# First stored weight set loaded inside the last block, third chunk's attention outputs moved by half a slot, two token sums made elsewhere

## The chip, the cores and the metric

One core of a Trainium2 chip runs the kernel. The metric is device time in microseconds (us) of one execution; the kernel before was timed three times. A profile is one execution more, with the start and length of every instruction on TensorE (PE, and PEld for its weight loads), VectorE (DVE), ScalarE (ACT), GpSimd (POOL) and the DMA issues of SyncE (SP).

## What is computed

```python
x = attention(q, k, v)          # 4 batches x 8 heads x 576 tokens x 64; heads 0-3: window 32,
                                # heads 4-7: 32 keys at a stride of 4; softmax; fp32
x = x as (2304 tokens, 512)
h = x @ w_in                    # 512 -> 2048
x = (h * sigmoid(h)) @ w_out    # 2048 -> 512
a, b = x @ w1, x @ w2           # 512 -> 1024 each
out = ((a * b) @ w3) @ w_out2   # 1024 -> 1024 -> 512
```

## The kernel before

Every fp32 operand of a large product is kept as two parts, an upper half (ScalarE's rounded copy) and a lower half (VectorE's difference), and a product is three matmuls: upper by upper, lower by upper, upper by lower. Weights arrive as 64-bit patterns and are converted on the chip: SP loads a piece of 512 KB into one of four `raw` buffers, ScalarE re-biases it, VectorE puts the bits together (two operations), ScalarE makes the upper half, VectorE the lower one. Each engine, SP too, works through its instructions in the order in which the program lists them; the order is written out by hand.

The tokens of the first feed-forward part go in five chunks, `CH1`, of 512, 512, 256, 512 and 512. For chunks 1 to 3 a *slot* (the loop after L1187) does one of 16 feature blocks: it makes `h` of the next block in two halves (`h` and `H` in the strings of `SLOT`, L72), the tanh and the gating (`t`), the halves of the gated block (`g`), and the product of the present block with `w_out` in two halves (`x` and `X`). An `a` in the string is one step of the attention of a later batch, eight steps per two heads' pair of units: outputs and scores (V, S), maxima on VectorE (M), exponentials (E, E), sums, GpSimd's multiplication and the copies into `xT` (N, O, L), transposes (T), and their copies out of PSUM (W). A slot has the string of the half in which the next step falls. A `p` is one operation out of a list of sums, `todo`.

Chunks 4 and 5 are computed together as a two by two block product with seven products instead of eight (`HPROD`, `h_product`, L863), which needs four sums of token blocks, T1 to T4; `t_ops` (L821) lists the operations that make them: raw sums `whole` into `x_a` to `x_d`, differences `sub`, and upper and lower halves `high` and `low`. T4 comes from `x_d`, T3 from `x_c`. The list `early` may run during the third chunk's attention, `late` in its last slots (string `SLOT[2]`), `last_` after them. Then the loop at L1324 runs eight pairs of seven products; the first pair does them in the order 0, 2, 4, 1, 3, 5, 6, with the last block's two `x` halves and the store of the third chunk (`x2_store`) between them, and product 0 is copied out of its bank twice (L1345). Four banks take turns. T1 is read by the third product, T2 by the fourth, T3 by the fifth, T4 by the sixth. During the later pairs three *sets* of the second part's weights (upper and lower halves of seven blocks) are made and stored to memory (`set_ops`), each 1.75 MB in two pieces (1024 and 768 KB).

The *last block* (loop at L1369) has 16 places of 12 matmuls for chunk 5, with up to seven conversion steps at each place (`LATE_MICROS`). At place 6 the tokens of the second part are loaded (`load_x2`, four loads of 384 KB). Then `weights(k, part)` (L1395) computes the product of `w3` and `w_out2`, 16 groups for the first half of the columns (k = 0 to 7), each of two parts of six matmuls, while the weights for the next groups are loaded and converted. The stored sets are read back there, at the values of k in `SET_AT` (L78) by `set_io` (L518), which issues two loads; they overwrite the tiles `wf[0]` to `wf[5]`, whose contents the last block read in places 6 to 11. After k = 8 the second part's products (`product`, L1045) begin, on two banks that the last groups' splits (L490) free.

Of the kernel before, what the change touches and what calls it, by code (L numbers as in the profile page):

```python
# [8 lines left out]
F32 = mybir.dt.float32  # L9
# [8 lines left out]
P = 128  # L18
# [11 lines left out]
PER_B = NPAIR * NU  # L30
# [40 lines left out]
ATT = "V2S0|M0|E1|E0|N0O3|L1O2|T0|W0"  # L71
SLOT = (  # L72
    ("ahapHppaxptapgX", "ahappHpxaptaXpg"),
    ("ahaHtapxgpaX", "ahHpaxtgpXaap"),
    ("phpHtxgpXpp",) * 2,
)
LATE_MICROS = 7
SET_AT = (1, 3, 6)  # L78
GROUP = ("mmmmw", "mmmmW")
MICROS = ("2223332", "3332121")  # L80
LAST = "00 01 02 20 21 13 22 14 33 34 15 35".split()
# [9 lines left out]
def tile_kernel(  # L91
# [650 lines left out]
    def x2_part(c, f, half):  # L742
        n = CH1[c][1]
        if f == 0 and half == 0:
            xps[c] = [ps_x.tile([P, 512], F32, tag="x", name=f"x2_{c}_{m}") for m in range(KT)]
        g = gt[c, f] if half == 0 else gt.pop((c, f))
        if half == 0 and type(g) is tuple:
            g = g[0]
        todo = [(m, sa, 0) for m in range(KT) for sa in (0, 1)] + [(m, 0, 1) for m in range(KT)]
        for m, sa, sb in todo[6 * half:6 * half + 6]:  # L750
            nc.tensor.matmul(  # L751
                xps[c][m][:, :n], wout(f, sa, m), g[:, sb],
                start=(f == 0 and sa == 0 and sb == 0), stop=(f == NF - 1 and sb == 1),
            )
# [66 lines left out]
    def t_ops():  # L821

        def tmp(k):
            if k not in tmps:
                tmps[k] = rawp.tile([P, 2, 512], F32, tag="raw", name=f"x_{k}")
            return tmps[k]

        def whole(k, r, c, kt):
            nc.vector.tensor_add(tmp(k)[:, kt], f32(x_block(r, c, 0, kt)), f32(x_block(r, c, 1, kt)))

        def sub(k, x, y, kt):
            nc.vector.tensor_sub(tmp(k)[:, kt], tmp(x)[:, kt], tmp(y)[:, kt])

        def view(n, k, kt):
            x = tmp(k)[:, kt]
            return x.rearrange("p (a n) -> p a n", a=2) if n == 3 else x

        def high(n, k, kt):
            nc.scalar.activation(t_block(n, 0, kt), view(n, k, kt), AF.Copy)

        def low(n, k, kt):
            nc.vector.tensor_sub(t_block(n, 1, kt), view(n, k, kt), f32(t_block(n, 0, kt)))

        two = lambda op, *z: [lambda kt=kt: op(*z, kt) for kt in range(2)]
        early = two(whole, "a", 0, 0) + two(whole, "b", 0, 1) + two(sub, "a", "b", "a")
        late = (two(high, 1, "a") + two(whole, "c", 1, 1) + two(low, 1, "a") + two(sub, "a", "c", "a") + two(high, 2, "a")
                + two(whole, "d", 1, 0) + two(low, 2, "a") + two(sub, "d", "d", "a") + two(high, 4, "d")
                + two(sub, "c", "c", "b") + two(low, 4, "d"))
        last_ = two(high, 3, "c") + two(low, 3, "c")
        return early, late, last_  # L850

    HPROD = [("11", "11"), ("S2", "T2"), ("12", "21"), ("S3", "T3"), ("S1", "T1"), ("22", "T4"), ("S4", "22")]
# [120 lines left out]
    def load_x2(pr):  # L973
        for half in range(2):
            for blk in range(2):
                t = x2p.tile([P, 2, T2], F32, tag=f"xb{half}{blk}", name=f"xb_{pr}_{half}{blk}")
                t0 = (2 * pr + blk) * T2
                nc.sync.dma_start(
                    out=t, in_=x2d[2 * half * P:(2 * half + 2) * P, t0:t0 + T2].rearrange("(m p) t -> p m t", p=P)
                )  # L980
                xb[f"{half + 1}{blk + 1}"] = t
# [155 lines left out]
    with tc.manual_schedule():  # L1137
# [50 lines left out]
        for i, (c, f) in list(enumerate(slots))[NF:-1]:  # L1188
            nxt = slots[i + 1]
            half = att.half()  # L1190
            if att.at == len(att.steps) and "T" not in tmps:
                attn.close()
                parts_ = ctx.enter_context(ExitStack())
                sp = parts_.enter_context(tc.tile_pool(name="sp", bufs=1, side="right", reuse_waits="tile"))
                tmps["T"] = [sp.tile([P, 2, 2, 512], F32R, tag=f"T{n}", name=f"T{n}") for n in range(2)]
                for u in (1, 2, 3):
                    load_sw(0, u)
                todo += late
            for x in SLOT[2 if "T" in tmps else c - 1][half]:
                if x == "h":  # L1200
                    if nxt[1] == 0:
                        att.need(2)
                    h_part(*nxt, 0)
                elif x == "H":
                    h_part(*nxt, 1)
                    if nxt[1] == NF - 1:
                        att.limit = (c + 3) * PER_B
                elif x == "t":
                    g_tanh(*nxt)
                    g_mul(*nxt)  # L1210
                elif x == "g":
                    g_high(*nxt)
                    g_low(*nxt)
                elif x in "xX":
                    x2_part(c, f, "xX".index(x))
                    if x == "X" and f == NF - 1:
                        x2_store(c, (0, 2))
                elif x == "a":
                    if att.half() == half:
                        att.step()  # L1220
                elif x == "p" and todo and (len(todo) > len(early) or c == 2 and (att.out >= 3 * PER_B + 6 or "T" in tmps)):
                    todo.pop(0)()
        load_sw(0, 0)
        for op in todo + last_:
            op()

        def gate(c):
# [96 lines left out]
        for p in range(NP):  # L1324
            if p == 1:
                bank = [ps_x.tile([P, 512], F32, tag="x", name=f"hx{k}") for k in range(4)]
                xps[3] = [(ps_h if m < 2 else ps_a).tile([P, 512], F32, tag="h" if m < 2 else "a", name=f"x2_3_{m}")
                          for m in range(KT)]
            for j, i in enumerate((0, 2, 4, 1, 3, 5, 6) if p == 0 else range(7)):
                live[i] = bank[done[0] % 4]  # L1330
                done[0] += 1
                h_product(p, i, live[i])
                if p == 0 and j < 2:
                    x2_part(2, NF - 1, j)
                    if j == 1:
                        x2_store(2, (0, 2))
                        raws = [rawp.tile([P, 2, 512], F32, tag="raw", name=f"c_{k}") for k in range(2)]
                        cs.update(s1=raws[0][:, 0], u2=raws[0][:, 1], u3=raws[1][:, 0], c22=raws[1][:, 1])
                        o = rawp.tile([P, 2, 2, 256], F32, tag="raw", name="set_out")
                        w = rawp.tile([P, 512, 2], I32, tag="raw", name="set_raw")  # L1340
                        t = sp.tile([P, 256], F32, tag="set_t", name="set_t")
                        sets = [op for s in range(SETS) for op in set_ops(s, t, w, o)]
                        ts.append(gp.tile([P, 512], F32, tag="t", name="t_s", bufs=1))
                        for k in ("s1", "u3"):
                            nc.scalar.activation(cs[k], live[0], AF.Copy)  # L1345
                elif p == 0:
                    begin_h(i)
                else:
                    collect_h(p, i)
                x_some(3, xs, 4 if i < 3 else 3, NF - 1)  # L1350
                for _ in range(2 if i in (1, 2, 3, 5, 6) else 1):
                    if sets and p:
                        sets.pop(0)()
            xs = first_x(p)
# [14 lines left out]
        for i, f in enumerate(LATE):  # L1369
            for z in x_todo():  # L1370
                x_mm(4, f, g_late(f), *z, first_=i == 0, last=i == NF - 1)
            cv2.allowed = sum(z <= i for z in free_at)
            if i == 6:
                load_x2(0)
            if i >= 8 and begin:
                begin.pop(0)()
            for _ in range(LATE_MICROS):
                cv2.micro()
# [16 lines left out]
        def weights(k, part):  # L1395

            if (k, part) == (3, 0):
                x2_store(NC1 - 1, (2,))
            if part == 0:
                cv2.allowed = W3[min(k + 1, 2 * NG - 1)] + 1  # L1400
                cv2.need(W3[k])
                if k < NG:
                    cv2.need(WO[k], False)
                if k in SET_AT:
                    set_io(SET_AT.index(k), False)
            for x in GROUP[part]:
                if x == "m":
                    cv2.micro()
                else:
                    wp_group(k, part)  # L1410
                    if todo:
                        x_split(todo.pop(0))
# [108 lines left out]
```

## Time and profile before

| | |
|---|---|
| time, three runs | 798.47, 798.94 (median), 800.08 us |
| the profiled execution | 800.56 us, of which the span of the trace is 798.8 us |
| TensorE (matmul) busy | 784.3 us, 98% |
| VectorE busy | 557.8 us, 70% |
| ScalarE busy | 346.0 us, 43% |
| GpSimd busy | 55.8 us, 7% |
| DMA | 120.93 MB, 151 GB/s in the mean, 370 GB/s in the busiest of 40 slices (479 to 499 us) |

Busy times are sums over instructions. A TensorE matmul starts before the modelled end of the one before it, so that its busy time hides small gaps. The chain of waits of the page goes through TensorE for nearly all of the span.

### The profile page before, as it was taken

The numbers are of one execution on the slowest core, as the hardware profiler recorded it, in microseconds if no ns is written. First come the engines' busy times: TensorE is split into PE (matmuls) and PEld (weight loads), VectorE is DVE, ScalarE is ACT, GpSimd is POOL, SyncE is SP. The second block draws the span as 40 slices with busy tenths as digits, with TensorE's granted clock in tenths as the row PEclk, the third lists the DMA queues.
The fourth block names the chain that finished last, engine by engine and source line by source line (L and its number), as shares of the span: only waits on it lengthen the run. The fifth ranks groups of instructions, "written<-read, shape, count | busy, mean of one in ns | idle before, by whom it ended". The sixth has DMA issues, their size and how long they took to land. (4 is left out here: it accounts for less than half of the span.)

```text
span 798.8 us, 13328 instructions
## 1 busy us (share of the span) xinstructions
PE 784.3 (98%) x4829; PEld 678.5 (85%) x4829; DVE 557.8 (70%) x1334; ACT 346.0 (43%) x868; POOL 55.8 (7%) x90
## 2 busy tenths in 40 slices
PE   7999999999999999999999999999999999999997
PEld 6788888888889897888888887889899999999996
DVE  5998892776765657878874857588877555774444
ACT  6877873554545534444433645343233211320111
POOL 4101100010100100000000000013300000000000
PEclk9999999999999999999999999999999999999999
DMA  9787740524235103455434859518522660045202
GB/s 240 230 275 230 215 147 16 195 96 168 83 130 172 56 15 106 137 166 159 145 119 156 275 223 370 174 54 324 229 93 68 207 251 2 1 152 204 93 1 79
DMA packets 54562, 120.93 MB, mean 151 GB/s; under 512 B 5089, under 2 KB 25313, under 8 KB 52449
## 3 DMA queue, kind: packets, MB, share of 16 engines
q1 hardware_dynamic: 54208, 119.85, 45.3%
q8 instruction: 38, 0.62, 0.3%
q10 hardware_dynamic: 288, 0.23, 0.1%
q14 instruction: 28, 0.22, 0.1%
HBM read 87.56 MB, written 32.51 MB: 150 GB/s over the span
## 5 line engine op out<-in xcount | busy, mean ns | idle before, releaser
L1045 PE MATMUL bank<-xT,wf 128*128 128x384 f32 x864 | 164.0, 335 | 0.5 <-DVE wf L493 0.4
L1045 PEld LDWEIGHTS bank<-xT,wf 128*128 128x128 f32 x864 | 151.7, 188 | 7.7 <-DVE wf L493 0.8
L751 PE MATMUL x<-g,wf 128*128 128x512 f32 (+1 forms) x576 | 121.9, 357 | 1.5 <-ACT g L734 1.5
L711 PE MATMUL h<-xT,wf 128*128 128x512 f32 (+1 forms) x576 | 120.9, 358 | 0.0
L1101 PE MATMUL o<-wf,wf 128*128 128x512 f32 x429 | 110.0, 393 | 0.0
L751 PEld LDWEIGHTS x<-g,wf 128*128 128x128 f32 x576 | 95.1, 189 | 17.4 <-ACT g L734 2.2
L711 PEld LDWEIGHTS h<-xT,wf 128*128 128x128 f32 x576 | 95.1, 189 | 15.8
L1101 PEld LDWEIGHTS o<-wf,wf 128*128 128x128 f32 x429 | 79.5, 188 | 12.7
L1081 ACT ACTIVATE wf<-c 128x384 fp32r<-128x384 f32 x48 | 25.2, 525 | 84.9 <-DVE c L1079 84.6
L1063 ACT ACTIVATE s<-bank 128x384 f32<-128x384 f32 x24 | 11.8, 491 | 103.0 <-PE bank L1045 92.4
L885 PE MATMUL x<-ga,wf 128*128 128x512 f32 x192 | 51.9, 391 | 0.0
L729 DVE SCALAR_TENSOR_TENSOR t<-t,h 128x512 f32<-128x512 f32 (+1 forms) x48 | 28.6, 595 | 33.4 <-ACT t L725 33.0
L690 PE MATMUL wp<-wf,wf 128*128 128x512 f32 x192 | 46.9, 392 | 0.3 <-ACT wf L602 0.3
L265 ACT ACTIVATE sm<-sm,nm 128x96 f32<-128x96 f32 x108 | 39.1, 365 | 17.4 <-DVE nm L255 17.3
L725 ACT ACTIVATE t<-h 128x512 f32<-128x512 f32 (+1 forms) x48 | 25.1, 522 | 47.3 <-PE h L711 45.6
L885 PE MATMUL x<-wf 128*128 128x512 f32 x192 | 43.7, 389 | 0.0
L739 DVE TENSOR_TENSOR g<-t,g 128x512 fp32r<-128x512 f32 (+1 forms) x48 | 28.8, 600 | 20.3 <-ACT g L734 19.9
L280 POOL TENSOR_TENSOR sm<-sm,rs 128x288 f32<-128x288 f32 x36 | 27.2, 764 | 225.7 <-DVE rs L275 67.3
L885 PEld LDWEIGHTS x<-ga,wf 128*128 128x128 f32 x192 | 36.0, 188 | 8.1
L1070 DVE TENSOR_TENSOR c<-u,bank 128x384 f32<-128x384 f32 x36 | 19.9, 552 | 32.7 <-PE bank L1045 32.6
L885 PEld LDWEIGHTS x<-wf 128*128 128x128 f32 x192 | 36.0, 188 | 7.5
L690 PEld LDWEIGHTS wp<-wf,wf 128*128 128x128 f32 x192 | 35.7, 188 | 7.7 <-ACT wf L602 0.8
(168 smaller groups left out, 1214.3 us busy)
## 6 DMA issues: line engine op xcount, KB each, us to landing
rawj<-in_w_dram SPq DMA_DIRECT2D x26, 512.0 KB, 5.9
wf<-setd SPq DMA_DIRECT2D x11, 1024.0 KB, 5.3
wf<-setd SPq DMA_DIRECT2D x11, 768.0 KB, 7.0
raw_i<-in_w_in_dram SPq DMA_DIRECT2D x16, 512.0 KB, 4.6
raw_u<-in_w_out_dram SPq DMA_DIRECT2D x16, 512.0 KB, 4.6
swd<-sw SPq DMA_DIRECT2D x16, 512.0 KB, 2.6
sw<-swd SPq DMA_DIRECT2D x24, 256.0 KB, 3.2
setd<-set_out SPq DMA_DIRECT2D x21, 256.0 KB, 2.1
```

The costliest lines, as they stand in the source:

```text
L265: nc.scalar.activation(sm[:, j], sm[:, j], AF.Exp, bias=nm[:, j:j + 1], scale=-1.0, accum_out=su[:, j:j + 1],)
L280: nc.gpsimd.tensor_tensor(sm, sm, rs[:, :NB].to_broadcast([P, NB, KB]), op=ALU.mult)
L690: nc.tensor.matmul(wp_ps[i], a[:, i // 2, sa, i % 2 * P:(i % 2 + 1) * P], o[:, sb], start=(jt == 0 and x == 0), stop=(jt == NG - 1 and x = ...
L711: nc.tensor.matmul(ps, win(f, sa, kt), xT[:, kt, sb, r0:r0 + n], start=(kt == 0 and x == 0), stop=(kt == KT - 1 and x == 2),)
L725: nc.scalar.activation(gt[c, f], hps[c, f][:, :n], AF.Tanh, scale=0.5)
L729: nc.vector.scalar_tensor_tensor(t, t, 1.0, ps, op0=ALU.add, op1=ALU.mult)
L739: nc.vector.tensor_sub(g[:, 1], t, f32(g[:, 0]))
L751: nc.tensor.matmul(xps[c][m][:, :n], wout(f, sa, m), g[:, sb], start=(f == 0 and sa == 0 and sb == 0), stop=(f == NF - 1 and sb == 1),)
L885: nc.tensor.matmul(xps[c][m], wout(f, sa, m), g[:, sb], start=(first_ and sa == 0 and sb == 0), stop=(last and sb == 1),)
L1045: nc.tensor.matmul(b, a_op(s, a, sa, kt), b_op(x, sb, kt), start=(n == 0), stop=(n == 5),)
L1081: behind.append((count[0] + 1, lambda: nc.scalar.activation(hi, c[k], AF.Copy)))
L1101: nc.tensor.matmul(ps, g_block(jj, n, sa)[:, m % 3 * P:(m % 3 + 1) * P], wp_v(f, sb)[:, c0:c1], start=((first_ or len(parts) == 2) and x = ...
```

## The change

Four edits. In the third chunk's slots with attention, the outputs and scores stand after the first half of `h` instead of before it, and the maxima after the second half (`SLOT[1][0]`). T4's raw sum goes from `late` to `early`, T4's halves go from `late` to a list that runs after the first of the 56 products, and T3's difference moves forward in `late`; `SLOT[2]` has three `p` instead of five. The copies of the first product out of its bank, and the buffers for them, stand right after that product instead of after the third chunk's store. The first set is loaded at place 11 of the last block instead of at k = 1, the second at k = 1 instead of 3, the third at k = 6 as before.

```diff
-    ("ahaHtapxgpaX", "ahHpaxtgpXaap"),
-    ("phpHtxgpXpp",) * 2,
+    ("haHatapxgpaX", "ahHpaxtgpXaap"),
+    ("hpHtxgpXp",) * 2,
...
-SET_AT = (1, 3, 6)
+SET_AT = (1, 6)
...
-        early = two(whole, "a", 0, 0) + two(whole, "b", 0, 1) + two(sub, "a", "b", "a")
+        early = two(whole, "a", 0, 0) + two(whole, "b", 0, 1) + two(sub, "a", "b", "a") + two(whole, "d", 1, 0)
         late = (two(high, 1, "a") + two(whole, "c", 1, 1) + two(low, 1, "a") + two(sub, "a", "c", "a") + two(high, 2, "a")
-                + two(whole, "d", 1, 0) + two(low, 2, "a") + two(sub, "d", "d", "a") + two(high, 4, "d")
-                + two(sub, "c", "c", "b") + two(low, 4, "d"))
-        last_ = two(high, 3, "c") + two(low, 3, "c")
+                + two(sub, "c", "c", "b") + two(low, 2, "a") + two(sub, "d", "d", "a"))
+        last_ = [two(high, n, k) + two(low, n, k) for n, k in ((3, "c"), (4, "d"))]
...
-                elif x == "p" and todo and (len(todo) > len(early) or c == 2 and (att.out >= 3 * PER_B + 6 or "T" in tmps)):
+                elif x == "p" and todo and (len(todo) > len(early) or c == 2 and (att.out >= 3 * PER_B + (6 if len(todo) > 2 else 10) or "T" in tmps)):
                     todo.pop(0)()
         load_sw(0, 0)
-        for op in todo + last_:
+        for op in todo + last_[0]:
             op()
...
                 if p == 0 and j < 2:
+                    if j == 0:
+                        raws = [rawp.tile([P, 2, 512], F32, tag="raw", name=f"c_{k}") for k in range(2)]
+                        cs.update(s1=raws[0][:, 0], u2=raws[0][:, 1], u3=raws[1][:, 0], c22=raws[1][:, 1])
+                        for k in ("s1", "u3"):
+                            nc.scalar.activation(cs[k], live[0], AF.Copy)
+                        for op in last_[1]:
+                            op()
                     x2_part(2, NF - 1, j)
                     if j == 1:
                         x2_store(2, (0, 2))
-                        raws = [rawp.tile([P, 2, 512], F32, tag="raw", name=f"c_{k}") for k in range(2)]
-                        cs.update(s1=raws[0][:, 0], u2=raws[0][:, 1], u3=raws[1][:, 0], c22=raws[1][:, 1])
...
-                        for k in ("s1", "u3"):
-                            nc.scalar.activation(cs[k], live[0], AF.Copy)
...
             if i == 6:
                 load_x2(0)
+            if i == 11:
+                set_io(0, False)
...
                 if k in SET_AT:
-                    set_io(SET_AT.index(k), False)
+                    set_io(SET_AT.index(k) + 1, False)
```

## Rows read from the trace of the kernel before

**Rows 1.** Timeline of TensorE, third chunk: start, length, operation, count, idle and releaser

```profile
239.81 0.82 PE L291 MATMUL t<-ident,sm 128*96 128x128 f32 x6
240.38 1.68 PE L711 MATMUL h<-xT,wf 128*128 128x256 f32 x12
...
251.14 1.60 PE L751 MATMUL x<-g,wf 128*128 128x256 f32 x12
252.58 0.89 PE L291 MATMUL t<-ident,sm 128*96 128x128 f32 x6
253.76 0.95 PE L315 MATMUL o<-at,v 96*64 96x64 f32 x24 [0.29 <-ACT at L302]
...
255.77 1.70 PE L711 MATMUL h<-xT,wf 128*128 128x256 f32 x12
257.31 1.60 PE L751 MATMUL x<-g,wf 128*128 128x256 f32 x12
```

**Rows 2.** Timelines of ScalarE and VectorE, the same two slots

```profile
253.24 0.85 ACT L302 ACTIVATE at<-t 96x384 f32<-96x384 f32 x2
257.51 0.38 ACT L725 ACTIVATE t<-h 128x256 f32<-128x256 f32 x1 [3.42 <-PE h L711]
...
256.40 0.25 DVE L255 CUSTOM_DVE_ANT_0 sm<-o,mask 128x96 f32<-128x96 f32 x1
```

**Rows 3.** Timeline of TensorE, last slots and first products

```profile
300.10 1.60 PE L711 MATMUL h<-xT,wf 128*128 128x256 f32 x12
302.66 1.69 PE L751 MATMUL x<-g,wf 128*128 128x256 f32 x12 [0.96 <-ACT g L734]
...
306.31 0.98 PE L751 MATMUL x<-g,wf 128*128 128x256 f32 x6 [0.57 <-ACT g L734]
...
312.59 1.66 PE L876 MATMUL hb<-xT,sw 128*128 128x512 f32 x6 [0.44 <-ACT c L1345]
```

**Rows 4.** Chain of waits, six matmuls of 512 columns: start, time to the next piece

```profile
502.01 1.39 PE wp L690 x6
```

**Rows 5.** Timelines of ScalarE and VectorE, last slots and first products

```profile
300.81 0.63 ACT L839 ACTIVATE xT<-x_d 128x512 fp32r<-128x512 f32 x1 [2.30 <-DVE x_d L832]
...
311.94 0.60 ACT L1345 ACTIVATE c<-hb 128x512 f32<-128x512 f32 x1 [1.72 <-DMA x2d<-x2s]
...
304.19 1.29 DVE L842 TENSOR_TENSOR xT<-x_d,xT 128x512 fp32r<-128x512 f32 x2
```

**Rows 6.** Timeline of TensorE, weight products and first set product

```profile
472.26 21.92 PE L690 MATMUL wp<-wf,wf 128*128 128x512 f32 x96
494.53 3.29 PE L690 MATMUL wp<-wf,wf 128*128 128x512 f32 x12 [0.35 <-ACT wf L602]
498.25 1.34 PE L1045 MATMUL bank<-xT,wf 128*128 128x384 f32 x6 [0.42 <-DVE wf L493]
```

**Rows 7.** Timelines of SP's queue and of ScalarE, weight products

```profile
484.49 4.34 SPq L545 DMA_DIRECT2D rawj<-in_w_dram  x3
...
493.29 0.67 ACT L553 ACTIVATE rawj<-rawj 128x512 f32<-128x512 f32 x1 [4.05 <-DMA rawj<-in_w_dram]
```

**Rows 8.** Busy time by stretch: last columns are clock, DMA share, GB/s

```profile
468.00:470.00 2.00, 2.00 (x11) 1.65 (x10) 0.93 (x1) 0.00 (x0) 0.00 (x0) 1.00 0.00 0
```

**Rows 9.** Timelines of GpSimd and VectorE, third chunk

```profile
269.82 1.74 POOL L280 TENSOR_TENSOR sm<-sm,rs 128x288 f32<-128x288 f32 x2 [7.90 <-ACT xT L334]
280.00 0.67 POOL L280 TENSOR_TENSOR sm<-sm,rs 128x288 f32<-128x288 f32 x1 [0.41 <-DVE rs L275]
...
270.08 0.96 DVE L832 TENSOR_TENSOR x_a<-x_b,x_a 128x512 f32<-128x512 f32 x1
281.15 0.43 DVE L739 TENSOR_TENSOR g<-t,g 128x256 fp32r<-128x256 f32 x1 [0.48 <-ACT g L734]
```

**Rows 10.** Timelines of SP's queue and TensorE, second pair of products

```profile
312.18 8.90 SPq L861 DMA_DIRECT2D sw<-swd  x4
...
319.18 1.55 PE L876 MATMUL hx<-T,sw 128*128 128x512 f32 x6
```

## Prediction

> **What bounds the kernel now.** I read the busy shares first: TensorE is busy for 784.3 us of a span of 798.8 us (table above). The change adds and removes no matmul, so it can only give back time in which TensorE stands or spaces its matmuls out. I then read TensorE's rows in order of time around each edit and took losses from the distance between two *starts*, not from the idle figure in brackets: a matmul's modelled end overlaps the next one's start, so the bracket understates a stop. TensorE stands in three places, and each edit meets one of them.
>
> First, the third chunk's attention [rows 1]. Twelve matmuls of 256 columns take 1.44 us from start to start (251.14 to 252.58). The transposes at 252.58 are followed directly by the attention outputs at 253.76, which is 1.18 us; where a half of `h` follows, the same six take 0.57 us (239.81 to 240.38). The outputs wait for the copies of the transposes out of PSUM, which ScalarE starts only at 253.24 [rows 2]. The pattern stands four times in the trace; its first case is in the rows.
>
> Second, the seam between the third chunk's last slots and the first products of the fourth and fifth [rows 3]. The second product of the last slot starts 2.56 us after `h` instead of 1.44 (300.10 to 302.66): 1.12 lost. From 302.66 to 306.31 are 3.65 us for 12 matmuls of 256 columns (1.44) and six of 512 (1.39 [rows 4]): 0.82 lost. From 306.31 to 312.59 are 6.28 us for twice six of 256 (0.72 each) and three times six of 512, which is 5.61: 0.67 lost. Sum 2.61 us. What ended last is in [rows 5]: ScalarE stood 2.30 us for `x_d` and then made T4's upper half, ahead of the tanh of the same slot; VectorE made T4's lower half at 304.19, ahead of the gating of the last block; and the copy of the first product out of its bank came at 311.94, behind a store of the third chunk that still held the copy's buffer.
>
> Third, the weight products [rows 6]. The 96 matmuls from 472.26 run 21.92 us; without the last one's overlap of 0.16 that is 21.76, or 1.36 per six. The next group could start at 494.02 and starts at 494.53: 0.51 lost. Its two sixes take 3.72 us instead of 2.72: 1.00 lost. Sum 1.51 us. The cause is in [rows 7]: a weight load that SP issued at 484.49, directly behind the second set (1.75 MB), kept ScalarE standing for 4.05 us until 493.29, 8.8 us after the issue; behind that stand, in ScalarE's order, come the upper half of the weights that TensorE wants at 494.02, and the splits that free the product banks.
>
> **The change part by part.** *The set loads.* The first set moves to place 11 of the last block. In SP's order it stands right behind four token loads and three weight loads, and nothing follows until the fifth chunk's first store, after the block. From 468 to 472 the DMA queues move nothing (two rows of 2 us, the first in [rows 8]), and from 466 on almost nothing; at the 370 GB/s of the busiest slice (table) 1.75 MB take 4.7 us, so the load ends about 471. What it overwrites was last read by places 6 and 7 of the block, which at 2.72 us a place end some 21 us before 472.26: SP doesn't stand for them. In the weight products the second set now takes the first one's place, the third set stays, and none is loaded between them. So the load issued at 484.49 has no set ahead of it; even at 5 us it lands at 489.5, 4.5 us before TensorE's wish at 494.02, and the loads behind it move up with it. What could be late next is the release of the banks: the last group ends at 494.02, a copy, a second copy beside the first subtraction and the second subtraction take at most 0.7 us each (0.63 and 0.65 for this size [rows 5]), so until 496.1, and the first set product is due at 496.74. Gain 1.5 us; bounded below by 0, if the supply of weights stays short.
>
> *The outputs half a slot further on.* The order becomes transposes, half of `h` (0.72 us, which hides the copies), outputs, scores, the other half of `h`. Removed: 1.18 − 0.57 = 0.61 us. Added: one or two more changes between narrow and full-width matmuls, for which the row is `h` after the scores, 1.54 instead of 1.44 (255.77 to 257.31) [rows 1], so 0.10 each. That leaves 0.41 to 0.61; I take 0.43, near the end with two changes, as the new order has two. Four times: 1.7 us (1.6 to 2.4). If the half of `h` did not cover the copies, the outputs would wait again and the 0.61 would shrink; ScalarE starts them 0.66 us after the transposes start and takes 0.43 each, so the first is out at 1.1 and the outputs start at about 1.5. The scores now come 0.8 us later in the slot. Their last maximum on VectorE ended at 256.65 [rows 2]; it will end about 0.1 us after the end of `h`, where the tanh starts at 0.2 and the exponentials queue behind it. So the softmax isn't late, with a margin of some 0.4 us.
>
> *The two token sums.* T4's raw sum moves to the end of the attention, its halves move behind the first product, and T3's difference goes forward in the slots. The last slots have two or three long operations instead of four or five, and those on VectorE stand behind the slot's own gating but one. VectorE's work in a slot is at most three of 0.6 us (1.29 for two [rows 5]) and 0.8 for the gate, of 2.88. The three stops lose their causes: no `x_d` ahead of the tanh, no T4 half ahead of the last gating, and the copies of the first product stand before the third chunk's store, on buffers whose readers are through. What is late next: T4 is wanted by the sixth product. Counted from the end of the last `h` that is 1.44 + 1.44 + 5 × 1.39, so 9.8 us; VectorE has by then two gate operations, a T2 half, two differences, two T3 halves and two T4 halves, which from 1.5 on at 0.6 each end at about 6. The copies end at about 4, and the bank is wanted again at 8.4. Gain 2.6 us; bounds 1.1 (only the first stop goes) and 2.9 (the delays of 0.1 in the slots before 300.10 go too).
>
> The moved raw sums could also meet GpSimd. Where such a sum ran beside the softmax multiplications, it took 0.96 us, and the two multiplications 1.74 instead of twice 0.67 (269.82, 270.08, 280.00) [rows 9]. The Trainium skill, "SBUF — State Buffer", section "Who interferes with whom", states that a VectorE operation with two SBUF inputs contends with a GpSimd operation that reads SBUF; those numbers agree. T4's raw sums come behind the gate's lower half at 281.15, and the multiplication of that slot ends at 280.67 [rows 9]. So I cost them at nothing; a collision would cost the 0.4 us by which the multiplications were longer, and the time would be 793.5.
>
> **Sum.** 1.5 + 1.7 + 2.6 = 5.8 us. The profiled execution took 800.56 us, 1.76 above its span and 1.62 above the median of 798.94; 5.8 us off the profiled one is 794.8, and the stops don't grow with that difference, so off the median it is 793.1 us.
>
> **The rivals.** *The weights stay short:* two sets and the weights still fill the queues. The first edit gives nothing: 794.6. For it speaks that the slice is the busiest of all; against it that 4.7 us of its load go, while the stand was 4.05. *A new wait at the seam:* T3 and T4, made later, hold up the last gating or the sixth product, and the gain of 2.6 shrinks to 1.1: 794.6. *The softmax comes late:* the maxima slip behind the tanh, the transposes wait for GpSimd by 0.4 each, and the 1.7 is gone: 794.8. *The set load isn't hidden:* if it goes ahead of the token loads or SP stands at it, the weights come late again, which is the first rival's time.
>
> *Slower than before:* the raw weights that are loaded behind the third chunk's store now take a buffer of that store, since the copies took the free ones. SP stands there until the store lands, in the trace at about 311.9 [rows 5], and the stored sums of the next pair stand behind it. The first that counts was issued at 312.18 for a product at 319.18 [rows 10]; now that is some 312.9 and, with 0.67 less standing, 318.5: 5.6 us to land. A load as slow as 8.8 us [rows 7] would cost 3.2 us (796.3). It eats the whole sum from 5.6 + 5.8 = 11.4 us on, and at 13.5 us the time is 801. Nothing fills the queues there, so I give it little.
>
> **How the numbers follow.** All three edits as summed: 0.62, by itself from 792.1 to 794.2. Weights short 0.10, a new wait at the seam 0.13, the softmax late 0.09, the slow landing 0.03, several of them 0.03. A measurement tells about 0.2% (1.6 us) from no change. Faster holds the first four cases, less a little for the worst of them: 0.90; within it 0.05; slower 0.05. The range goes from 791.6, with 2.4 and 2.9 for the second and third term, to 795.8, with one edit lost and half of another.
>
> **What the profile after would show.** Right would be: outputs about 2.2 us after the transposes start, with `h` between and no wait for the copies; 1.44 us from `h` to the second product through the last slot, and no stop in the first seven products; no stand of ScalarE for weights near 490, and the first set product 2.7 us after the second half's first group; the queues busy from 466 to 471. Wrong would be a stop at a new place in one of these stretches, above all at the sixth product or the first products of the next pair, or a stand for weights that has only moved.

## The result and the profile after

| | before | after |
|---|---|---|
| time, median of 6 runs each | 799.15 us (798.47 to 801.78) | 792.27 us (791.64 to 794.25) |
| ratio | | 0.9913, 95% interval 0.9896 to 0.9931 |
| profiled execution, span | 800.56, 798.8 us | 792.24, 790.4 us |
| TensorE busy | 784.3 us | 782.6 us |

Forecast were 793.1 us and 791.6 to 795.8. To see where the time went I cut both spans at the same instructions on TensorE, from start to start (us; "seam" is split at the first product, and the last column begins at the first group of the last product):

```
                 start-up  to 3rd     third     seam   seam   first pairs  weight    to the   to the
                           chunk    attention    1      2     to last blk  products  output   end
before             29.92   209.89     44.15    20.23  14.07     154.00      25.99     36.28   264.27
after              28.34   209.92     42.50    18.71  12.51     154.11      24.48     36.17   263.66
```

The edits give 1.65 in the third chunk's attention, 1.52 + 1.56 = 3.08 at the seam and 1.51 in the weight products: 6.24 us. The rest of the 8.4 us between the spans is start-up (1.58), which no edit touches, the last stretch (0.61, see the end) and -0.03 in the others.

Timeline of TensorE after, the slot that answers to [rows 1]:

```profile
251.02 0.89 PE L291 MATMUL t<-ident,sm 128*96 128x128 f32 x6
251.66 0.96 PE L711 MATMUL h<-xT,wf 128*128 128x256 f32 x6
252.55 0.92 PE L315 MATMUL o<-at,v 96*64 96x64 f32 x24
```

The outputs start 1.53 us after the transposes, with half of `h` between, and show no bracket (idle time and what ended it): TensorE doesn't wait for the copies. Timeline of TensorE after, last slots and first products [rows 3]:

```profile
296.59 1.60 PE L711 MATMUL h<-xT,wf 128*128 128x256 f32 x12
298.03 1.60 PE L751 MATMUL x<-g,wf 128*128 128x256 f32 x12
299.47 1.55 PE L875 MATMUL hb<-xT,wf 128*128 128x512 f32 x6
300.86 0.88 PE L751 MATMUL x<-g,wf 128*128 128x256 f32 x6
301.57 1.55 PE L875 MATMUL hb<-xT,wf 128*128 128x512 f32 x6
302.96 0.88 PE L751 MATMUL x<-g,wf 128*128 128x256 f32 x6
...
306.43 1.56 PE L875 MATMUL hb<-xT,sw 128*128 128x512 f32 x6
307.83 1.53 PE L875 MATMUL hb<-xT,wf 128*128 128x512 f32 x6
```

From the last `h` to the second product of its slot are 1.44 us (before 2.56); from there on every step has its length without a stop, 1.44 for twelve of 256 columns, 0.71 for six, 1.36 to 1.40 for six of 512. Timelines of ScalarE, then VectorE after, same stretch [rows 5]:

```profile
301.06 0.60 ACT L1337 ACTIVATE c<-hb 128x512 f32<-128x512 f32 x1
302.36 0.60 ACT L1337 ACTIVATE c<-hb 128x512 f32<-128x512 f32 x1 [0.71 <-DVE x_d L832]
```

```profile
303.51 1.29 DVE L842 TENSOR_TENSOR xT<-x_d,xT 128x512 fp32r<-128x512 f32 x2
304.72 0.75 DVE L766 TENSOR_SCALAR x2s<-x 128x256 f32<-128x256 f32 x2
```

The first product is copied out at 301.06, and the second time at 302.36, before the store; T4's lower half ends at 304.80, 3.0 us ahead of the sixth product at 307.83. VectorE's copies for the third chunk's store (`x2s`) come only behind it, from 304.72 on; what that costs is told below. Weight products after, TensorE, then ScalarE [rows 6, 7]:

```profile
466.09 24.64 PE L690 MATMUL wp<-wf,wf 128*128 128x512 f32 x108
490.57 1.23 PE L1044 MATMUL bank<-xT,wf 128*128 128x384 f32 x6
```

```profile
482.97 0.66 ACT L553 ACTIVATE rawj<-rawj 128x512 f32<-128x512 f32 x1
```

All 108 matmuls are one row, the set product follows 24.48 us after the start, and until then ScalarE doesn't stand for raw weights (the first such stand, of 0.81 us, ends at 493.65). The first set, SP's queue and busy time by stretch after [rows 8]:

```profile
451.72 1.32 SPq L522 DMA_DIRECT2D wf<-setd  x2
```

```profile
460.00:462.00 2.00, 2.00 (x10) 1.66 (x9) 1.48 (x2) 0.00 (x0) 0.00 (x0) 1.00 0.82 337
462.00:464.00 2.00, 2.00 (x10) 1.68 (x9) 0.00 (x0) 0.00 (x0) 0.00 (x0) 1.00 0.12 49
```

It is issued 14.4 us before the first weight product, shares full queues with the weight loads ahead of it, and the queues, down to a share of 0.12 from 462 to 464, move nothing more from 463.3 on, 2.8 us before the weight products begin.

### The profile page after: what moved, and what is told of

Same layout as the page of the kernel before. It is cut to its first block, busy times and chain, and to the rows that moved or that the text cites. A ratio compares the mean times of both kernels' runs of the same rounds, so it can differ in the third digit from the quotient of the medians.

```text
span 790.4 us, 13331 instructions
## 1 busy us (share of the span) xinstructions
PE 782.6 (99%) x4829; PEld 679.7 (86%) x4829; DVE 557.3 (71%) x1334; ACT 345.7 (44%) x868; POOL 57.1 (7%) x90
## 4 chain that ended last, share of the span: by engine, by line
PE 97%; DVE 1%; POOL 0%; ACT 0%; issue 0%; DVEq 0%; POOLq 0%
PE bank L1044 22%; PE h L711 14%; PE x L751 14%; PE o L1100 13%; PE x L884 11%; PE hx L875 9%; PE wp L690 6%; PE o L235 2%; PE o L315 2%; PE t L291 2%; PE hb L875 1%; PE s L235 1%; PE warm L1169 0%; POOL stage L280 0%; DVE stage L255 0%
## 5 line engine op out<-in xcount | busy, mean ns | idle before, releaser
L729 DVE SCALAR_TENSOR_TENSOR t<-t,h 128x512 f32<-128x512 f32 (+1 forms) x48 | 28.6, 595 | 30.2 <-ACT t L725 29.8
L280 POOL TENSOR_TENSOR sm<-sm,rs 128x288 f32<-128x288 f32 x36 | 27.2, 764 | 224.4 <-DVE rs L275 66.5
```

The costliest lines, as they stand in the source:

```text
L280: nc.gpsimd.tensor_tensor(sm, sm, rs[:, :NB].to_broadcast([P, NB, KB]), op=ALU.mult)
L729: nc.vector.scalar_tensor_tensor(t, t, 1.0, ps, op0=ALU.add, op1=ALU.mult)
```

## Experiments

Every time stands beside runs of the kernel before on the same chip (medians 799.46, 799.31 and 799.11 us for the three groups of runs). Stretches are those of the table above.

**The changed kernel again.**

> The changed kernel itself, to compare the others with. From start to start the trace after shows 1.6 us less in the third chunk's attention (four times 0.4), 3.1 us less from the last slots to the second pair of products, 1.6 us less in the weight products, together 6.3 us. Theory (three separate stops are gone): 6.3 us less than before, 0.9921 of it, and the start of the first products of the third chunk differs between executions by more than a microsecond without any edit, because the first inputs land differently. Rival (part of the gain lies elsewhere, at the start or behind the set products): 7.5 us or more less.

793.51 us, ratio 0.9929 (0.9917 to 0.9941). Stretches 42.50, 18.72, 12.51, 24.48, and 263.67 at the end: all as in the profile after, to 0.01. The start-up was 29.13 instead of 28.34, and the way to the third chunk 210.46 instead of 209.92.

**One edit undone at a time.** The sets back:

```diff
-SET_AT = (1, 6)
+SET_AT = (1, 3, 6)
-            if i == 11:
-                set_io(0, False)
-                    set_io(SET_AT.index(k) + 1, False)
+                    set_io(SET_AT.index(k), False)
```

> The changed kernel with the three set loads where they were (k = 1, 3, 6). Theory (that edit alone ends the stop in the weight products): the stop of 1.5 to 1.6 us is back between the first half's last group and the first set product, ScalarE stands about 4 us for weights there, the other two stretches are as in the changed kernel, so 1.6 us slower than the changed kernel. Rival (the weights come earlier because the earlier edits shifted the work before them): no stop, no difference.

795.47 us, 0.9955 (0.9938 to 0.9972). Weight products 26.35, which is 1.87 more; all else as in the changed kernel. Timelines of SP, ScalarE and TensorE:

```profile
479.37 1.23 SPq L522 DMA_DIRECT2D wf<-setd  x2
480.69 4.34 SPq L545 DMA_DIRECT2D rawj<-in_w_dram  x3
```

```profile
489.88 0.65 ACT L553 ACTIVATE rawj<-rawj 128x512 f32<-128x512 f32 x1 [4.44 <-DMA rawj<-in_w_dram]
```

```profile
491.10 3.29 PE L690 MATMUL wp<-wf,wf 128*128 128x512 f32 x12 [0.72 <-ACT wf L602]
494.81 1.31 PE L1044 MATMUL bank<-xT,wf 128*128 128x384 f32 x6 [0.43 <-DVE wf L493]
```

The chain of the prediction is back link by link: set, load right behind it, stand of 4.44 us until 489.88, late upper half, late bank. The 1.87 are 0.36 more than the edit gave; the weights come 21.4 us after the start of the weight products, where they came at 21.0 in the kernel before, and why is open.

The slot back:

```diff
-    ("haHatapxgpaX", "ahHpaxtgpXaap"),
+    ("ahaHtapxgpaX", "ahHpaxtgpXaap"),
```

> The changed kernel with outputs and scores ahead of the first half of h again. Theory (the half of h covers the copies, at a price of 0.1 us for each change between narrow and full-width matmuls): transposes to outputs 1.18 us with a wait for the copies, four times, 1.6 us slower than the changed kernel. Rival (the copies are as late again, relative to the outputs, because ScalarE and VectorE follow TensorE): the outputs wait in the changed kernel as well and the difference is under 0.5 us.

795.17 us, 0.9945 (0.9933 to 0.9957). Attention 44.15, exactly the 1.65 back, and the four waits for the copies with it; the first (TensorE):

```profile
254.01 0.89 PE L291 MATMUL t<-ident,sm 128*96 128x128 f32 x6
255.19 0.95 PE L315 MATMUL o<-at,v 96*64 96x64 f32 x24 [0.29 <-ACT at L302]
```

The seam back: T4's list and the copies as before, sets and slot as changed.

> The changed kernel with the token sums and the copies of the first product as before; set loads and the order in the attention slots stay changed. Theory: the three stops of 1.1, 0.8 and 0.7 us and the small delays ahead of them are back, 3.1 us slower than the changed kernel. Rival (the stops come from the attention being late and are shorter now): under 1.5 us slower.

795.25 us, 0.9954 (0.9941 to 0.9967). Seam 20.23 and 14.07, exactly the 3.08 back. The median is only 1.74 above that of the changed kernel; its profiled run had the shortest start-up of all (27.22), so that I trust the stretches more than the medians, but whether start-up explains the other runs too isn't known.

**Place or amount of the set loads.** The second set goes to k = 3, still only two sets among the weight products:

```diff
-SET_AT = (1, 6)
+SET_AT = (3, 6)
```

> The changed kernel, but the second set is loaded at k = 3, right ahead of the weight load that kept ScalarE standing before; the first set stays in the last block. It tells two readings of the set edit apart. Theory of the place (what counts is that no set stands right ahead of that load): the load lands some 8 us after its issue again, ScalarE stands some 4 us, and the stretch from the first weight product to the first set product is 25.9 us again instead of 24.5. Theory of the amount (what counts is that 1.75 MB are out of the weight products): the queues have less behind them, the load lands in under 5.5 us, and the stretch stays at 24.5 us. The whole time would be 1.5 us above the changed kernel, or the same.

794.39 us, 0.9938 (0.9918 to 0.9958). Weight products 24.94, between the two theories: 0.46 of 1.51 is back. Timelines of ScalarE and TensorE:

```profile
487.12 0.66 ACT L553 ACTIVATE rawj<-rawj 128x512 f32<-128x512 f32 x1 [3.03 <-DMA rawj<-in_w_dram]
```

```profile
467.12 24.64 PE L690 MATMUL wp<-wf,wf 128*128 128x512 f32 x108
492.06 1.31 PE L1044 MATMUL bank<-xT,wf 128*128 128x384 f32 x6 [0.31 <-DVE wf L493]
```

The load right behind the set is late again (a stand of 3.03 us), but its weights are re-biased 20.0 us after the weight products start instead of 21.0 in the kernel before [rows 6, 7] and 21.4 with all three sets back. That is in time for the matmuls and only the bank is late. So a set ahead of a load makes the stand, and the set less at k = 1 takes most of its price away: both count.

**The seam in two.** T4's halves back into the slots, copies as changed:

```diff
-    ("hpHtxgpXp",) * 2,
+    ("phpHtxgpXpp",) * 2,
...
-        early = ... + two(whole, "d", 1, 0)
+        late = ... + two(whole, "d", 1, 0) ... + two(high, 4, "d") ... + two(low, 4, "d")
```

> The changed kernel, but T4's raw sum and halves, and the five places for sums in a slot, are as before; the copies of the first product stay where the change put them. Theory (T4's work ahead of the tanh and the gating causes the first two stops): the stretch from the end of the attention outputs to the first product is 20.2 us again instead of 18.7, the stop of 0.7 to 0.8 us ahead of the last block's x is back, no stop ahead of the fifth product: 2.2 to 2.4 us slower than the changed kernel. Rival (the stops need both the sums and the copies): under 1 us slower.

795.49 us, 0.9947 (0.993 to 0.9964). Seam 20.23 and 13.34: the first two stops are back, with 1.52 and 0.83. TensorE:

```profile
298.12 1.60 PE L711 MATMUL h<-xT,wf 128*128 128x256 f32 x12
300.69 1.70 PE L751 MATMUL x<-g,wf 128*128 128x256 f32 x12 [0.97 <-ACT g L734]
...
304.33 0.98 PE L751 MATMUL x<-g,wf 128*128 128x256 f32 x6 [0.56 <-ACT g L734]
```

From the third chunk's last half of `x` (306.54) to the issue of its store (307.70) are 1.16 us, as in the kernel before (308.52 to 309.68).

The copies back behind the store, T4 as changed:

```diff
-                    if j == 0:
-                        raws = ...; cs.update(...)
-                        for k in ("s1", "u3"):
-                            nc.scalar.activation(cs[k], live[0], AF.Copy)
...
                         x2_store(2, (0, 2))
+                        raws = ...; cs.update(...)
...
+                        for k in ("s1", "u3"):
+                            nc.scalar.activation(cs[k], live[0], AF.Copy)
```

> The changed kernel, but the two copies of the first product, and their buffers, stand behind the third chunk's store again; T4's halves stay behind the first product. Theory (the copies' place and buffers cause the third stop alone): a stop of about 0.6 us ahead of the fifth product, where the bank is wanted, and the store's landing named as what the copy waited for; first two stops stay away; from the first product to the second pair's first x 13.1 us instead of 12.5. Rival (the third stop was only the tail of the first two): 12.5 us.

793.69 us, 0.9923 (0.9907 to 0.994). The second part of the seam takes 14.23, so this stop alone costs 1.72, nearly three times what was expected. That rests on the profiled run, 794.98 us; the other three took 793.66 to 793.71, close to the changed kernel's 793.51 on another chip, and how long their start-up was isn't known. ScalarE, TensorE and SP, then TensorE and SP in the kernel before, from the third chunk's last half of `x` (304.00, 308.52) on:

```profile
308.44 0.60 ACT L1347 ACTIVATE c<-hb 128x512 f32<-128x512 f32 x1 [2.03 <-DMA x2d<-x2s]
```

```profile
304.00 0.88 PE L751 MATMUL x<-g,wf 128*128 128x256 f32 x6
...
306.10 1.53 PE L875 MATMUL hb<-T,sw 128*128 128x512 f32 x6
309.08 1.66 PE L875 MATMUL hb<-xT,sw 128*128 128x512 f32 x6 [1.46 <-ACT c L1347]
```

```profile
306.18 0.88 SPq L767 DMA_DIRECT2D x2d<-x2s  x2
```

```profile
308.52 0.88 PE L751 MATMUL x<-g,wf 128*128 128x256 f32 x6
```

```profile
309.68 0.88 SPq L767 DMA_DIRECT2D x2d<-x2s  x2
```

ScalarE stands 2.03 us for the store that holds the copy's second buffer, and the fifth product waits for that copy. In the kernel before the same stop cost 1.56 - 0.83 = 0.73. The difference of 0.99 comes from T4's move: its halves now stand on VectorE ahead of the copies that the store sends. From the start of that half of `x` to the store's issue are 2.18 us here (304.00 to 306.18) and 2.24 in the changed kernel (302.96 to 305.20), but 1.16 in the kernel before (308.52 to 309.68) and in the two with T4 in its old place. The copy that waits for the store, and the product behind it, are later by the same 1.0 us. So the copies' new place is worth 0.73 in the sum, and it also takes away 0.99 that T4's move alone would have added.

**The margin of the softmax.** The outputs another half of `h` further:

```diff
-    ("haHatapxgpaX", "ahHpaxtgpXaap"),
+    ("hHaatapxgpaX", "ahHpaxtgpXaap"),
```

> The changed kernel, but outputs and scores stand behind the whole of h, half a slot later again. The change left the softmax a margin that I put at 0.4 us, and this takes 0.8 us more. Theory (margin as estimated): the maxima now end after the tanh, the exponentials and GpSimd's multiplications come 0.5 to 0.9 us later, and TensorE waits at the transposes by 0.4 to 0.9 us, in three or four places: the third chunk's attention takes 44.0 to 45.5 us instead of 42.5. Rival (the softmax has more room than that): 42.5 us or a little less, as one change between narrow and full-width matmuls falls away.

791.96 us, 0.99 (0.9885 to 0.9915). Attention 41.83, 0.67 *less*. The prediction's margin of 0.4 us would have been overrun; no transpose comes later, and from transposes to transposes, two slots, it takes 8.58 us (251.02 to 259.60) instead of 8.66. Narrow and full-width matmuls change as often as in the changed kernel; what is shorter is the way from the transposes to `h`, 0.57 instead of 0.64. GpSimd's second multiplication ends 0.30 us after the first of these transposes starts in the changed kernel (250.65 + 0.67 = 251.32) and ahead of it here (250.26 + 0.67 = 250.93), so that a short wait for it is likely; the trace names none. Of the 0.67, 0.11 reappears in the first part of the seam (18.82 instead of 18.71), where the change behind the last outputs now falls: the net gain is 0.56. The stop at the third transposes, which the kernel before has too (0.47 at 271.62), is smaller here. TensorE, changed kernel, then this one:

```profile
266.88 1.60 PE L751 MATMUL x<-g,wf 128*128 128x256 f32 x12
268.32 0.49 PE L291 MATMUL t<-ident,sm 128*96 128x128 f32 x3
269.28 0.53 PE L291 MATMUL t<-ident,sm 128*96 128x128 f32 x3 [0.47 <-POOL sm L280]
269.57 0.96 PE L711 MATMUL h<-xT,wf 128*128 128x256 f32 x6
```

```profile
268.18 1.13 PE L291 MATMUL t<-ident,sm 128*96 128x128 f32 x6
269.06 1.67 PE L711 MATMUL h<-xT,wf 128*128 128x256 f32 x12
```

From the transposes to `h` are 1.25 and 0.88 us, where it takes 0.64 and 0.57 in the other slots.

**What the stop at the third transposes is.** VectorE's long sums are moved away from the reciprocals and from GpSimd's multiplications:

```diff
-    ("haHatapxgpaX", "ahHpaxtgpXaap"),
+    ("haHatapxgaX", "ahHaxtgpXaappp"),
```

> The changed kernel with the sums of the third chunk's slots laid out otherwise: the `p` ahead of the last `X` of SLOT[1][0] is gone and SLOT[1][1] is "ahHaxtgpXaappp", so that no two-input operation of VectorE on SBUF tiles runs beside GpSimd's multiplications in the first slots of an attention unit. It asks what the 0.47 us are for which TensorE stands at the third transposes of the changed kernel (269.28), waiting for GpSimd, and which stand nowhere else in that chunk. Theory, the two engines share something: the multiplications take 0.67 each again instead of 1.74 for two, the stop goes, the third chunk's attention takes 41.9 to 42.0 instead of 42.50, and the time is 0.5 to 0.6 us lower (ratio 0.9921 where the changed kernel has 0.9928). Rival, GpSimd starts late because VectorE's sums or ScalarE's copies come late there, whatever runs beside it: the stop and 42.50 stay.

793.17 us, 0.9928 (0.991 to 0.9946). Attention 41.91, 0.59 less, and nothing in brackets (transposes to `h` 0.65). GpSimd in the changed kernel, then here, and TensorE here:

```profile
267.48 1.74 POOL L280 TENSOR_TENSOR sm<-sm,rs 128x288 f32<-128x288 f32 x2 [7.51 <-ACT xT L334]
```

```profile
266.53 0.67 POOL L280 TENSOR_TENSOR sm<-sm,rs 128x288 f32<-128x288 f32 x1 [6.91 <-DVE rs L275]
267.60 0.67 POOL L280 TENSOR_TENSOR sm<-sm,rs 128x288 f32<-128x288 f32 x1 [0.40 <-DVE rs L275]
```

```profile
266.52 1.60 PE L751 MATMUL x<-g,wf 128*128 128x256 f32 x12
267.96 0.89 PE L291 MATMUL t<-ident,sm 128*96 128x128 f32 x6
```

Counted from the start of the product half ahead of the transposes (266.88, 266.52), the multiplications ran from 0.60 to 2.34 and run from 0.01 to 1.75. Both theories hold a part. The first multiplication began 0.6 us late because a raw sum stood ahead of the reciprocals on VectorE: with twice 0.67 it would still have ended at 1.94, 0.2 late. The other 0.40 is the stretching beside a two-input sum, 1.74 instead of 1.34. The edit takes both away at once; they were not tried apart.

Both edits together, and the two yardsticks beside them:

```diff
-    ("haHatapxgpaX", "ahHpaxtgpXaap"),
+    ("hHaatapxgaX", "ahHaxtgpXaappp"),
```

> Both: the whole of `h` ahead of the outputs and the scores ("hHaatapxgaX") and the sums of the third chunk away from GpSimd's multiplications. Either edit alone takes away the stop at the third transposes, if the stop is the only thing that each of them gives; then the attention takes 41.8 as with the first alone and nothing is added (ratio 0.9918). Rival, the slots are each shortened by the earlier outputs and the contention costs elsewhere too: 41.2 to 41.5 (0.9911 to 0.9914).

> The kernel with the whole of `h` ahead of the outputs, a second time, beside the changed kernel on the same chip: attention 41.83, time 0.6 to 0.7 us below the changed kernel's (ratio to it 0.9992). If the 0.3 to 1.5 us by which it was lower before came from the start-up, the two agree.

> The changed kernel once more, unedited, as the yardstick for the three beside it: attention 42.50, seam 18.71 and 12.51, weight products 24.48, ratio to the kernel before 0.991 to 0.993. What its start-up until the first block's 21st half of `h` differs from 28.3 and 29.1 us is no effect of any edit.

Together 792.36 us, 0.9918 (0.9898 to 0.9937), attention 41.52, between the two theories: the whole of `h` first had left 0.31 of the stop (0.88 for 0.57), and exactly that is gone. Nothing else in these slots is shorter. The kernel with the whole of `h` first took 792.25 us, 0.9917 (0.9899 to 0.9935), attention 41.84, as expected; the changed kernel 793.62 us, 0.9937 (0.9919 to 0.9955), stretches 42.51, 18.71, 12.51, 24.48. With the 0.11 that each has more in the seam (18.82 and 18.81), the stretches say that both variants beat the changed kernel, by 0.87 and 0.56 us; their medians lie 1.3 and 1.4 below it, with intervals that overlap.

**The slow landing.** In the last yardstick the way from the seam to the last block took 155.06 instead of 154.11. TensorE at the second pair of products, the changed kernel and its yardstick, and the SP issue in each:

```profile
312.89 1.66 PE L875 MATMUL hx<-T,sw 128*128 128x512 f32 x6
```

```profile
314.11 1.65 PE L875 MATMUL hx<-T,sw 128*128 128x512 f32 x6 [0.82 <-DMA sw<-swd]
```

```profile
305.20 0.88 SPq L767 DMA_DIRECT2D x2d<-x2s  x2
307.39 0.35 SPq L898 DMA_DIRECT2D set_raw<-in_w_dram  x1
...
308.31 2.80 SPq L860 DMA_DIRECT2D sw<-swd  x3
```

```profile
308.53 2.81 SPq L860 DMA_DIRECT2D sw<-swd  x3
```

This is the mechanism of the prediction's slower case. SP's next issue comes 1.3 us after the end of the store's (306.08 to 307.39; before 310.56 to 310.61), and the profile names the store's landing as what SP waited for. It issues the stored sums at 308.31, and the product wants them at 312.89, 4.6 us later (before 7.0 [rows 10]). Of the 2.4 us, 1.1 are the later store, 0.6 are SP's way from the store to the stored sums (3.11 instead of 2.50), and 0.7 are the third stop, gone between the third chunk's last `x` and the product. With T4 in its old place and the copies as changed the lead was 5.7 us (310.80 to 316.48). The slowest of the eight loads in this stretch landed in 4.7 us here and in 5.7 us in the yardstick, where the product waited 0.82 us. Of the twelve profiles with the seam edit whole or in part, four show the wait (0.85, 0.6, 0.2, 0.82 us); the two of the old seam don't.

## Why the prediction was right, and where not

**The set loads**, 1.5: measured 1.51, and 1.87 when undone in the changed kernel. The cause named, a load behind a set, is shown by the two experiments. Wrong in the detail: I put the load at 466 to 471; on the clock of the kernel before (6.2 us more) it ran from 457.9 to about 469.4, longer than the 4.7 us of its bytes, since weight loads shared the queues. It cost nothing, since nothing was wanted earlier.

**The outputs half a slot further**, 1.7 (four times 0.43): 1.65, so 0.41 each. The outputs start 1.53 after the transposes, as worked out (1.5); the 2.2 in the list of what the profile would show contradicts that and was a slip. The margin of 0.4 us for the softmax was a step that failed without harm: I took the maxima and the tanh behind them for the next limit, and another half of `h` made the stretch shorter.

**The two token sums**, 2.6: 3.08, the one term that was mis-sized. Its three stops were put at 1.12, 0.82 and 0.67; undone apart, they give 1.52, 0.83 and 0.73 in the sum. The excess of 0.4 in the first lies around it: delays of 0.31 in the slots ahead of 300.10, which I had only in the upper bound, at 0.3, went as well, and 0.09 behind it. What I had not seen is that T4's halves, behind the first product, hold up the third chunk's store by 1.1 us. By itself that would have made the third stop 1.72; it cost nothing in the sum because the copies moved as well. What was to be late next held: T4 ends 6.8 us after the last `h` (put at 6), wanted at 9.8; the second copy ends at 4.9 (put at 4), wanted at 8.4.

**GpSimd's collision**, at nothing for the moved sums: right, T4's raw sums run from 278.70, after that slot's last multiplication has ended (277.20 + 0.67 = 277.87). But the same collision stood unpriced in the kernel before, at the third transposes [rows 9]; with the sum ahead of the reciprocals it is worth 0.6 us. The Trainium skill, "SBUF — State Buffer", section "Who interferes with whom", calls the pair of ports an exclusive lock; the trace shows both operations stretched (0.68 to 0.96, 1.34 to 1.74) and still over one another: 2.02 us of work in the 1.74 from 267.48 on. Neither was held off for the whole of the other.

**The slower case** got 0.03 and its mechanism is real, at an eighth of the size that would have turned the sign (0.8 against some 6 us). My 5.6 us to land were 4.6, because I left the store where it was, ahead of SP's stand; counted from the third chunk's last `x`, it went out 1.1 us later.

**The sum**: 6.24 by the stretches against 5.8. The lower end of the range was a slip: 798.94 less 1.5 + 2.4 + 2.9 is 792.1, not 791.6; the measured 792.27 lies above both. The three medians of the changed kernel lie 6.9, 6.0 and 5.5 us below those of the kernel before beside them.

## What to carry to other kernels

Read a loss from start to start around the place. When an operation is moved, look at what stands behind it in its new place: T4's halves, taken away from the gating, stood ahead of the copies for a store, the store went out 1.1 us later, and the stop that hung on it would have grown from 0.73 to 1.72 without the second edit. When an operation moves ahead of a store, look at what SP then finds in its queue: here a buffer that was free before made SP stand. Both together, and the stop that was gone, took 2.4 us of lead from a load, and it came too late in some executions. A stop that the change doesn't name, like that of the third transposes, is worth pricing beside it: moving two sums there gave 0.59 us, a fifth of the change's third term.

## What was not expected of the hardware

The start-up, until the first unbroken row of 21 matmuls of `h`, took from 27.2 to 31.3 us over the fourteen profiles, and 28.3, 29.1 and 28.6 in three of one and the same kernel. The spread over all of them is larger than what any single edit gave, so that a difference between two profiles' spans says little until it is cut at instructions.

In the last stretch VectorE stands 0.46 us at one place in the two kernels with the old seam and in none of the twelve others, and TensorE's next row of bank matmuls starts about 0.2 us later there. The whole stretch took 264.27 and 264.11 in these two and 263.56 to 263.98 in the others, so that part of the 0.61 is scatter. VectorE, kernel before:

```profile
575.71 0.55 DVE L1070 TENSOR_TENSOR s<-u,bank 128x384 f32<-128x384 f32 x1 [0.46 <-PE bank L1045]
```

The instructions around it are the same in all. In the kernel before the bank's matmuls begin 1.61 us ahead of this addition, in the changed kernel 1.25 us ahead. Why is open.
